# Backward loads on another queue, a gradient product with exchanged operands, a residual on GpSimd, and a tail in two steps

## The chip, the core and the metric

The kernel runs on one core of a Trainium2 chip. A core has five engines with instruction queues of their own, each worked off strictly in order: PE (TensorE, matrix products; its weight loads are shown apart as PEld), DVE (VectorE), ACT (ScalarE), POOL (GpSimd) and SP (SyncE, which computes nothing and issues DMAs). SP, ACT and POOL can issue DMAs; the transfers then run on the core's 16 DMA engines. An instruction that waits for a semaphore holds up everything behind it on its own engine. The metric is the device time of one launch in microseconds (us); lower is better. The profile is of one execution of the same program, with every instruction, semaphore and DMA packet.

## The reference

One block of a transformer, forward and backward, in bfloat16, with S = 2048 rows, width D = 448, 16 heads of 28, and F = 1792:

```
xn  = layernorm(x)
y   = x + MHA(xn; wqkv, wo) + SwiGLU(xn; w_gate, w_up, w_down)
out = y and, for a given grad_out, the gradients of
      x, wqkv, wo, w_gate, w_up, w_down
```

MHA is softmax attention over all rows with scale 28^-0.5; SwiGLU is (silu(xn w_gate) * (xn w_up)) w_down. The seven outputs are y, dx, d(wqkv), d(wo), d(w_gate), d(w_up), d(w_down), in that order.

## The kernel before

The program has three phases, one behind the other on every engine.

**Forward phase** (up to 655 us). For each of 4 groups of 4 heads, scores are made in transposed form by PE, exponentiated by ACT (L605) and multiplied with v. The whole feed-forward part, its gradients and the gradients of its weights are spread between these steps by a small work queue. What the backward phase needs goes to DRAM scratch: qT_d, kT_d, vT_d, dOT_d (per group, transposed), spq_d, spk_d, spo_d (per group, rows on partitions), hd_d (the three hidden tensors h, dgate, dup per row tile), wT_d and wqT_d (transposed weights). POOL issues nearly all of these stores.

**Backward phase** (655 to 1472 us). It runs over 512 units: 8 pairs of heads, 4 key blocks of 512, 16 query tiles of 128. One unit k is: scores on PE (L852), E = exp on ACT (L870), dP on PE for the unit before (L863), ds = dP * E on DVE (L881), and, three units later, the products that accumulate dk and dv on PE (acc_mm, L749). Eight units form a window W (so 64 windows); `pos` is a unit's place in its window. dq needs ds transposed: for 6 of a window's 8 units SP issues a transposing DMA dsT<-ds (L883), for the other two PE transposes (L776) and ACT or DVE copies out (L783). Two windows later dq_mm (L796) multiplies and DVE adds up (L808 to L814). ds lies in 8 rotating buffers (pool dsw), so a ds can be written only when the transposing DMA and the products of the unit eight before it are done.

Finished dk/dv blocks (dkv_o, L755) and dq blocks (dq_o, L814) are transposed back by a DMA from SP into dkv_sp and dq_sp (L762, L818) and stored to dqkv_d by POOL (L764, L821). These issues stand in a list `sp_later` and are emitted after the dsT of the next unit.

**Jobs.** Each window also carries at most one job of PE work from the list `jobs` (L650), in four portions at pos 1 to 4 between the unit's own products ("fillers"): 16 jobs "y" (a row tile of y: 4 + 14 products and one with the identity that adds x, L713 and L715), 32 jobs "dx" (a row tile of dgate or dup times the transposed weight, 14 products, L719) and 12 jobs "dwq" (4 chunks of 128 rows of d(wqkv), for each of the first three groups; 64 small products each, L677 and L682, with xn as the stationary operand and dkv_sp or dq_sp as the moving one). A job's result is copied out of PSUM by ACT (L728, L692) and stored by POOL (L730, L732); for a dwq job POOL first sorts the columns with 6 copies (L699). The fourth group's dwq products run at the end of the phase, in `last_dwq`.

**Loads of the phase**, all issued by SP, in the same queue as the transposing DMAs: the chunk ck of hd_d (and x_c) for the job two windows ahead, at pos 0 (L661, L663, L667; 3 buffers); at pos 4 parts of the next pair's qT and kT (8 parts of 128 KB over four windows, L553), of the next group's v_sp, vT, O_sp (6 parts of 256 KB over six windows, L564), and of the next weight W (parts of 224 KB, two a window, L540, one buffer).

**Tail** (1472 to 1548 us). Three `load_c` on SP bring the first pieces of pA_d, pB_d and dqkv_d (L937, L940), the rest is issued by ACT. After the last dwq products, 16 row tiles t of dx follow: 14 products on PE (L957, L959), a copy with a row sum on ACT (L963), the layer norm's gradient on DVE (L966 junk with a row sum, L970 bb, L972 cc), t1 on ACT (L975), t2 on DVE (L977), the addition of dy on POOL (L980) and the store by SP (L981).

Of the kernel before, what the change touches and what calls it, by code (L numbers as in the profile page):

```python
# [18 lines left out]
D = 448  # L19
# [18 lines left out]
def kernel(  # L38
# [493 lines left out]
    def load_w(nm, parts):  # L532
# [6 lines left out]
        q = pool if nm == "wd" else sp  # L539
        out = [lambda i=i: q.dma_start(out=t[:, i:i + step, :], in_=src[:, i:i + step, :])  # L540
# [5 lines left out]
    def load_pair(pr, parts):  # L546
# [6 lines left out]
        return [lambda i=i, dst=dst, r0=r0, src=src: sp.dma_start(  # L553
# [4 lines left out]
    def load_group(g, parts, kpool):  # L558
# [5 lines left out]
        return [lambda i=i, t=t, src=src: sp.dma_start(  # L564
# [65 lines left out]
    outp = cst.enter_context(tc.tile_pool(name="outp", bufs=2))  # L630
    ps_sd = cst.enter_context(tc.tile_pool(name="ps_sd", bufs=3, space=PSUM))
# [15 lines left out]
    chunk, dsp, dqacc = {}, {}, {}  # L647


    jobs = [None] + [("y", t) for t in range(NT)] + [None] + [("dwq", 0, c) for c in range(4)]  # L650
    jobs += [("dx", 0, t) for t in range(NT)] + [("dwq", 1, c) for c in range(4)]
    jobs += [("dx", 1, t) for t in range(8)] + [None] + [("dwq", 2, c) for c in range(4)]
    jobs += [("dx", 1, t) for t in range(8, NT)]

    def job_load(i):
# [3 lines left out]
        if j[0] == "y":  # L659
            t = ckp.tile([P, NFC + G, P], BF16, name="ck")  # L660
            sp.dma_start(out=t[:], in_=hd_d[j[1], :, :G + NFC, :])  # L661
            x = ckp.tile([P, D], BF16, name="x_c")
            sp.dma_start(out=x[:], in_=x_d[:, j[1], :])  # L663
            chunk[i] = (t, x)
        elif j[0] == "dx":
            t = ckp.tile([P, NFC + G, P], BF16, name="ck")
            sp.dma_start(out=t[:, :NFC], in_=hd_d[j[2], :, G + NFC * (1 + j[1]):G + NFC * (2 + j[1]), :])  # L667
            chunk[i] = t

    def dwq_mms(g, c, ps):  # L670

        out = []
        lhs = lambda t: xn_sp[:, t, c * P:(c + 1) * P]

        def kvm(t):
            for hp in range(2):
                pe.matmul(ps[:, hp * P:(hp + 1) * P], lhsT=lhs(t), rhs=dsp[2 * g + hp][0][:, t, :],  # L677
                          start=(t == 0 and hp == 0), stop=(t == NT - 1), skip_group_check=True)

        def qm(t):  # L680
            for hp in range(2):
                pe.matmul(ps[:, 256 + hp * 64:256 + hp * 64 + 64], lhsT=lhs(t),  # L682
                          rhs=dsp[2 * g + hp][1][:, t // 8, t % 4, t % 8 // 4, :],
                          start=False, stop=(t == NT - 1), skip_group_check=True)
        for f in (kvm, qm):
            out.append([lambda t=t, f=f: f(t) for t in range(NT)])
        return out

    def dwq_out(g, c, ps):
        d0, dn = DCH[c]  # L690
        o = outp.tile([P, 384], BF16, name="dwq_raw")
        act.copy(out=o[:], in_=ps[:, :384])  # L692
        z = outp.tile([P, 3, 4, DH], BF16, name="dwq_z")
        kv = o[:, :256].rearrange("p (h v j r) -> p h v j r", h=2, v=2, r=HP)
        for tq in range(3):
            for hp in range(2):
                src = (o[:, 256 + 64 * hp:320 + 64 * hp].rearrange("p (j r) -> p j r", r=HP) if tq == 0
                       else kv[:, hp, 2 - tq])
                pool.tensor_copy(out=z[:, tq, 2 * hp:2 * hp + 2, :], in_=src[:, :, :DH])  # L699
        pool.dma_start(  # L700
            out=out_2[d0:d0 + dn, :].rearrange("p (t c) -> p t c", t=3)[:, :, g * 4 * DH:(g + 1) * 4 * DH],
            in_=z[:dn].rearrange("p t h d -> p t (h d)"))

    def job_mms(i, ps):
        j = jobs[i]
        if j[0] == "dwq":
            return sum(dwq_mms(j[1], j[2], ps), [])
        if j[0] == "y":
            t, x = chunk[i]
# [303 lines left out]
```

## Time and profile before

| what | time |
|---|---|
| median of 3 runs (lowest, highest) | 1548.89 us (1547.53, 1555.15) |
| the profiled execution, and its span | 1549.43 us, 1547.7 us |
| granted PE clock, mean of the span | 0.978 |

Stages of the backward phase and the tail, from the busy time of each stretch. A window begins with the first E (L870) of its eight units; the period of a window is the distance to the next such start, read from the timeline of ACT.

| stage | windows | from, to (us) | length | PE busy | DVE busy | DMA, GB/s | shortest to longest window |
|---|---|---|---|---|---|---|---|
| y | 1 to 16 | 667.3, 883.8 | 216.5 | 193.5 | 169.1 | 205 | 12.23 to 16.67 |
| no job | 17 | 883.8, 894.6 | 10.8 | 9.3 | 10.4 | 187 | 10.8 |
| dwq, group 0 | 18 to 21 | 894.6, 952.4 | 57.8 | 48.9 | 42.6 | 203 | 11.85 to 17.18 |
| dx, gate | 22 to 37 | 952.4, 1156.0 | 203.6 | 189.1 | 169.8 | 202 | 11.76 to 16.01 |
| dwq, group 1 | 38 to 41 | 1156.0, 1204.0 | 48.0 | 46.1 | 42.4 | 193 | 11.88 to 12.15 |
| dx, up, first 8 | 42 to 49 | 1204.0, 1305.3 | 101.3 | 91.1 | 84.4 | 196 | 11.78 to 14.31 |
| no job | 50 | 1305.3, 1316.2 | 10.9 | 9.1 | 10.4 | 211 | 10.9 |
| dwq, group 2 | 51 to 54 | 1316.2, 1364.3 | 48.1 | 46.1 | 42.5 | 178 | 11.88 to 12.15 |
| dx, up, last 8 | 55 to 62 | 1364.3, 1459.6 | 95.3 | 92.0 | 85.0 | 195 | 11.78 to 12.15 |
| last window, start of the tail | 63 | 1459.6, 1494.5 | 34.9 | 28.1 | 14.1 | 248 | |
| rows of dx | | 1494.5, 1547.7 | 53.2 | 42.8 | 30.5 | 184 | |

"Busy" of PE is the time in which at least one product is under way. A window's period against the shortest ones of the same kind of job tells how much it lost; the DMA rate tells how much was moved in it. POOL is busy for 22.6 us of the 216.5 us of stage y and sits idle for the rest.

### The profile page before, as it was taken

What the parts mean: (1) busy time and instruction counts of PE and PEld (TensorE: products, weight loads), DVE (VectorE), ACT (ScalarE), POOL (GpSimd) and SP (SyncE); (2) the same over time, 40 slices, a digit from 0 to 9 for tenths busy, and PEclk for the clock granted to TensorE, in tenths of its full rate; (3) what the DMA queues carried; (4) which work ended last, traced back from release to release, by engine and by line L of the source; (5) the groups of instructions that cost most, each with busy time, mean ns of one, the idle gap of its engine ahead of it and who ended that gap; (6) DMA issues with size and microseconds to landing.
All of it is one profiled execution on the core that took longest, in us unless ns stands there. A gap on an engine that the chain in (4) does not pass through costs nothing.

```text
span 1547.7 us, 32024 instructions
## 1 busy us (share of the span) xinstructions
PE 1412.8 (91%) x12176; PEld 597.7 (39%) x12176; DVE 1099.4 (71%) x1421; ACT 1187.9 (77%) x1333; POOL 396.1 (26%) x664
## 2 busy tenths in 40 slices
PE   6899999999999989988988988989999889999987
PEld 3333333333333333433433444433335333543353
DVE  7654555656666657476877877878878789888935
ACT  6898988888788878676767867878778778888724
POOL 4341433343435355310110111111102101111033
PEclk9999999999999999999999999999999999999999
DMA  9985758767978689799999999999999999999994
GB/s 225 189 174 113 157 101 173 161 142 141 179 154 164 148 173 215 159 205 200 214 204 206 196 199 205 198 200 198 207 197 197 200 192 197 174 192 215 188 274 142
DMA packets 682106, 285.12 MB, mean 184 GB/s; under 512 B 637136, under 2 KB 650464, under 8 KB 681952
## 3 DMA queue, kind: packets, MB, share of 16 engines
q1 hardware_dynamic: 652016, 210.03, 74.6%
q0 software_dynamic: 25968, 64.53, 16.8%
q10 hardware_dynamic: 3968, 8.52, 1.6%
q8 instruction: 95, 1.56, 0.4%
q14 instruction: 59, 0.48, 0.1%
HBM read 67.34 MB, written 63.44 MB: 85 GB/s over the span
## 4 chain that ended last, share of the span: by engine, by line
PE 56%; DMA 13%; ACT 13%; DVE 8%; issue 6%; SPq 1%; POOL 1%; ACTq 0%; DVEq 0%; POOLq 0%
DMA dsT<-ds 9%; PE f_ps L357 7%; PE sd L852 6%; PE s_ps L600 6%; PE f_ps L383 6%; ACT E L870 5%; PE aux L719 4%; PE acc L749 4%; PE aux L796 4%; PE aux L776 4%; PE o_ps L582 4%; ACT eT L605 4%; DVE ds L881 3%; ACT dsT L783 3%; PE aux L713 3%
## 5 line engine op out<-in xcount | busy, mean ns | idle before, releaser
L881 DVE TENSOR_TENSOR ds<-sd,E 128x1024 bf16<-128x1024 f32 x512 | 611.4, 1220 | 137.5 <-DMA dsT<-ds 52.6
L870 ACT ACTIVATE E<-sd 128x1024 bf16<-128x1024 f32 x512 | 516.9, 1024 | 178.4 <-PE sd L863 140.2
L605 ACT ACTIVATE eT<-s_ps 128x1024 bf16<-128x1024 f32 x512 | 495.8, 1026 | 93.1 <-PE s_ps L600 89.6
L852 PE MATMUL sd<-kT,qT 32*128 32x512 bf16 x1024 | 201.8, 390 | 24.7 <-DVE ds L881 22.3
L863 PE MATMUL sd<-kT,qT 32*128 32x512 bf16 x1024 | 202.6, 389 | 23.6 <-ACT E L870 22.7
L749 PE MATMUL acc<-ds,v_sp 128*32 128x512 bf16 x1024 | 204.6, 395 | 0.7 <-DVE ds L881 0.7
L749 PE MATMUL acc<-E,O_sp 128*32 128x512 bf16 x1024 | 204.3, 395 | 0.2 <-ACT dkv_o L755 0.2
L600 PE MATMUL s_ps<-qT,kT 32*128 32x512 bf16 x1024 | 148.0, 386 | 7.8 <-ACT eT L605 5.6
L422 POOL DMA_DIRECT2D hd_d<-fT x168 | 126.9, 769 | 15.5 <-DVE fT L407 6.8
L383 PE MATMUL f_ps<-xnT,wgu 128*128 128x512 bf16 x448 | 118.8, 383 | 4.9 <-DVE w_sb L409 4.7
L764 POOL DMA_DIRECT2D dqkv_d<-dkv_o x64 | 39.3, 619 | 289.1 <-ACT dkv_o L755 287.3
L719 PE MATMUL aux<-W,ck 128*128 128x448 bf16 x448 | 108.4, 359 | 3.4
L852 PEld LDWEIGHTS <-qT 32*128 32x128 bf16 x1024 | 51.3, 91 | 154.1 <-issue 145.5
L582 PE MATMUL o_ps<-eT,v_sp 128*32 128x512 bf16 x1024 | 103.4, 394 | 0.6
L357 PE MATMUL f_ps<-xn_sp,f_sp 128*128 128x448 bf16 x448 | 99.1, 354 | 0.0
L749 PEld LDWEIGHTS <-O_sp 128*32 128x32 bf16 x1024 | 50.4, 94 | 113.4 <-issue 103.4
L600 PEld LDWEIGHTS <-kT 32*128 32x128 bf16 x1024 | 40.7, 91 | 137.7 <-issue 132.7
L776 PE MATMUL aux<-ident_bf,ds 128*128 128x128 bf16 x1024 | 79.4, 221 | 11.2 <-DVE dq_acc L808 5.8
L863 PEld LDWEIGHTS <-qT 32*128 32x128 bf16 x1024 | 65.4, 91 | 62.1 <-issue 58.2
L357 PEld LDWEIGHTS <-f_sp 128*128 128x128 bf16 x672 | 58.2, 98 | 77.4 <-issue 23.4
L776 PEld LDWEIGHTS <-ds 128*128 128x128 bf16 x1024 | 61.8, 98 | 39.8 <-issue 39.4
L395 DVE SCALAR_TENSOR_TENSOR g<-t_sb,f_ps 128x512 f32<-128x512 f32 x56 | 38.4, 686 | 53.3 <-ACT t_sb L393 53.2
(133 smaller groups left out, 1766.5 us busy)
## 6 DMA issues: line engine op xcount, KB each, us to landing
hd_d<-fT POOLq DMA_DIRECT2D x168, 128.0 KB, 4.4
ck<-hd_d SPq DMA_DIRECT2D x32, 448.0 KB, 4.4
ck<-hd_d SPq DMA_DIRECT2D x16, 576.0 KB, 5.1
dsT<-ds SPq DMA_TRANSPOSE x384, 4.2
dqkv_d<-dkv_o POOLq DMA_DIRECT2D x64, 64.0 KB, 3.8
dq_c<-dqkv_d ACTq DMA_DIRECT2D x5, 768.0 KB, 6.5
W<-wT_d SPq DMA_DIRECT2D x14, 224.0 KB, 3.6
out_dram<-dw_o POOLq DMA_DIRECT2D x28, 96.0 KB, 4.0
```

Source lines behind the costliest of these rows:

```text
L357: pe.matmul(acc[:, :D], lhsT=src[:, 12 * (t // 4) + 4 * wi + t % 4, :], rhs=rhs[:, t, :D], start=(t == 0), stop=(t == NT - 1))
L383: pe.matmul(st[name][:], lhsT=w(c), rhs=src[:, tsl, c, :], start=(c == 0), stop=(c == 3))
L582: pe.matmul(o_ps[HP * hh:HP * (hh + 1), :], lhsT=v[:, kt, HP * hh:HP * (hh + 1)], rhs=e[hh // 2][:, hh % 2, :], start=(kt == 0), stop=(kt ...
L600: pe.matmul(s_ps[:, j, :], lhsT=kT[r:r + HP, kt * P:(kt + 1) * P], rhs=qT[r:r + HP, qc * 512:(qc + 1) * 512], start=True, stop=True, tile_ ...
L605: act.activation(out=e[:], in_=s_ps[:], func=ACT.Exp, scale=SCALE)
L719: return [lambda n=n: pe.matmul(ps[:, :D], lhsT=t[:, n, :], rhs=w[:, n, :], start=(n == 0), stop=(n == NFC - 1)) for n in range(NFC)]
L749: pe.matmul(acc[r:r + HP, :], lhsT=src[:, qt, 64 * hp + HP * j:64 * hp + HP * j + HP], rhs=m[:, j, :], start=(qt == 0), stop=(qt == NT - 1 ...
L776: pe.transpose(ps[:, i, :], ds[:, i // 4, (i % 4) * P:(i % 4 + 1) * P], ident_bf[:])
L852: pe.matmul(s_ps[:, j, :], lhsT=q[HP * j:HP * j + HP, qt * P:(qt + 1) * P], rhs=kv[HP * j:HP * j + HP, kc * 512:(kc + 1) * 512], start=Tru ...
L863: pe.matmul(d_ps[:, j, :], lhsT=q[r:r + HP, qt * P:(qt + 1) * P], rhs=kv[r:r + HP, kc * 512:(kc + 1) * 512], start=True, stop=True, tile_p ...
L870: act.activation(out=E[k][:], in_=s_ps[:], func=ACT.Exp, scale=SCALE)
L881: dve.tensor_tensor(out=DS[k - 1][:], in0=d_ps[:], in1=E[k - 1][:], op=ALU.mult)
```

## The change

Five edits, made together.

1. Every load of the backward phase is issued by POOL and no longer by SP: ck and x_c, the pairs, the groups, and all weights. That includes the first pair and the first group, which are loaded near the end of the forward phase (L611).
2. dwq: for the first three groups, 3 jobs of 16 or 64 products each take the place of 4 jobs of 64. dkv_sp of one pair (c = 0, 1) or dq_sp of both pairs (c = 2) is the stationary operand, 448 columns of xn the moving one, so the result is the gradient transposed, 128 x 448. For c = 2 the operand is used in four pieces of 32 columns, each in its own column strip of PE. ACT copies the result to a bf16 tile with 64 zero columns, SP transposes it back by DMA, POOL sorts the columns (5 copies a group in all) and, with the third job, issues the four stores.
3. The list of jobs is 3 shorter; the windows without a job are now 0, 17, 40 and 60 to 63. The dwq jobs of group 2 now stand in windows 50 to 52, with 9 of the second "dx" jobs before them.
4. y: the product with the identity is left out. ACT copies PSUM to an fp32 tile, POOL adds x and writes the bf16 row that it then stores.
5. Tail: the last group's dwq is three results, each copied and transposed in turn after its products. In the loop over t, t2, the addition and the store (`finish`) of tile t - 1 follow t1 of tile t; the additions of the last three tiles are made by DVE.

```diff
@@ load_w, load_pair, load_group, job_load
-        q = pool if nm == "wd" else sp
-        out = [lambda i=i: q.dma_start(out=t[:, i:i + step, :], in_=src[:, i:i + step, :])
+        out = [lambda i=i: pool.dma_start(out=t[:, i:i + step, :], in_=src[:, i:i + step, :])
...
-        return [lambda i=i, dst=dst, r0=r0, src=src: sp.dma_start(
+        return [lambda i=i, dst=dst, r0=r0, src=src: pool.dma_start(
...
-            sp.dma_start(out=t[:], in_=hd_d[j[1], :, :G + NFC, :])
+            pool.dma_start(out=t[:], in_=hd_d[j[1], :, :G + NFC, :])
...
@@ jobs
-    jobs = [None] + [("y", t) for t in range(NT)] + [None] + [("dwq", 0, c) for c in range(4)]
-    jobs += [("dx", 0, t) for t in range(NT)] + [("dwq", 1, c) for c in range(4)]
-    jobs += [("dx", 1, t) for t in range(8)] + [None] + [("dwq", 2, c) for c in range(4)]
-    jobs += [("dx", 1, t) for t in range(8, NT)]
+    jobs = [None] + [("y", t) for t in range(NT)] + [None] + [("dwq", 0, c) for c in range(3)]
+    jobs += [("dx", 0, t) for t in range(NT)] + [("dwq", 1, c) for c in range(3)] + [None]
+    jobs += [("dx", 1, t) for t in range(9)] + [("dwq", 2, c) for c in range(3)]
+    jobs += [("dx", 1, t) for t in range(9, NT)]
@@ dwq_mms, dwq_out
         def kvm(t):
-            for hp in range(2):
-                pe.matmul(ps[:, hp * P:(hp + 1) * P], lhsT=lhs(t), rhs=dsp[2 * g + hp][0][:, t, :],
-                          start=(t == 0 and hp == 0), stop=(t == NT - 1), skip_group_check=True)
+            pe.matmul(ps[:, :D], lhsT=dsp[2 * g + c][0][:, t, :], rhs=xn_sp[:, t, :D],
+                      start=(t == 0), stop=(t == NT - 1))
         def qm(t):
-            for hp in range(2):
-                pe.matmul(ps[:, 256 + hp * 64:256 + hp * 64 + 64], lhsT=lhs(t),
-                          rhs=dsp[2 * g + hp][1][:, t // 8, t % 4, t % 8 // 4, :],
-                          start=False, stop=(t == NT - 1), skip_group_check=True)
+            for h in range(4):
+                pe.matmul(ps[HP * h:HP * (h + 1), :D],
+                          lhsT=dsp[2 * g + h // 2][1][:, t // 8, t % 4, t % 8 // 4, HP * (h % 2):HP * (h % 2 + 1)],
+                          rhs=xn_sp[:, t, :D], start=(t == 0), stop=(t == NT - 1),
+                          tile_position=(0, HP * h), skip_group_check=True)
+        return [lambda t=t: (kvm if c < 2 else qm)(t) for t in range(NT)]
...
+        w = dwq_w[c % 2]
+        act.copy(out=w[:, :D], in_=ps[:, :D])
...
+        def later():
+            sp.dma_start_transpose(out=o[:], in_=w[:])
+            parts = [(0, 0, 4, 0)] if c == 2 else [(2, 2 * c, 2, 0), (1, 2 * c, 2, 64)]
+            for tq, h0, n, c0 in parts:
+                pool.tensor_copy(out=z[:, :, tq, h0:h0 + n, :],
+                                 in_=o[:, :, c0:c0 + HP * n].rearrange("p c (h r) -> p c h r", r=HP)[:, :, :, :DH])
+            if c < 2:
+                return
+            for i, (d0, dn) in enumerate(DCH):
+                pool.dma_start(
...
+        sp_later.append(later)
@@ y
-            out.append(lambda: pe.matmul(ps[:, :D], lhsT=ident_bf[:], rhs=x[:], start=False, stop=True))
...
+        if j[0] == "y":
+            y = outp.tile([P, D], FP32, name="y_sb")
+            act.copy(out=y[:], in_=ps[:, :D])
+            pool.tensor_tensor(out=o[:], in0=y[:], in1=chunk[i][1][:], op=ALU.add)
+        else:
+            act.copy(out=o[:], in_=ps[:, :D])
@@ tail
+        for c, (ps, m) in enumerate(last_dwq):
+            for f in m[12 if c < 2 else 0:]:
+                f()
+            dwq_out(3, c, ps)
+            while sp_later:
+                sp_later.pop(0)()
...
+        def finish(t, t1, cc):
+            t2 = wk.tile([P, D], FP32, name="t2")
+            dve.scalar_tensor_tensor(out=t2[:], in0=xn_sp[:, t, :D], scalar=cc[:, 0:1], in1=t1[:],
+                                     op0=ALU.mult, op1=ALU.add)
+            dx = wk.tile([P, D], BF16, name="dx")
+            add = pool if t < NT - 3 else dve
+            add.tensor_tensor(out=dx[:], in0=t2[:], in1=dy_t[:, t, :], op=ALU.add)
+            sp.dma_start(out=out1_d[:, t, :], in_=dx[:])
...
+            if t > 0:
+                finish(t - 1, *held)
+            held = (t1, cc)
+        finish(NT - 1, *held)
```

## The prediction

> **What bounds the kernel now.** I read the page first (busy shares, chain, groups, DMA issues), then the start of every eighth L870 for the window periods, then the waits of the slow windows, then SP's queue as a timeline.
>
> ```profile
> DMA dsT<-ds 9%; PE f_ps L357 7%; PE sd L852 6%; PE s_ps L600 6%; PE f_ps L383 6%; ACT E L870 5%; PE aux L719 4%; PE acc L749 4%; PE aux L796 4%; PE aux L776 4%; PE o_ps L582 4%; ACT eT L605 4%; DVE ds L881 3%; ACT dsT L783 3%; PE aux L713 3%
> L881 DVE TENSOR_TENSOR ds<-sd,E 128x1024 bf16<-128x1024 f32 x512 | 611.4, 1220 | 137.5 <-DMA dsT<-ds 52.6
> dsT<-ds SPq DMA_TRANSPOSE x384, 4.2
> ```
>
> PE leads with 91% busy, yet the largest single item of the chain is a transfer, the transposing DMA dsT. DVE's ds waits 52.6 us for it: the buffer that ds wants has not been read yet. The chain in order of time places those pieces in windows that the table above shows as long. An undisturbed window takes 12.5 us with a y job, 11.9 with dx (11.78 and 12.05 in turn), 12.0 with dwq, 10.85 with none. Against that, stage y loses 216.5 - 16 x 12.5 = 16.5 us, the dwq of group 0 57.8 - 48.0 = 9.8, the first dx stage 203.6 - 16 x 11.92 = 12.9, the first half of the second 101.3 - 8 x 11.92 = 5.9, the rest nothing. Sum: 45 us of stalls. SP's queue in one slow window:
>
> ```profile
> 799.86 0.79 SPq L661 DMA_DIRECT2D ck<-hd_d  x1
> 800.75 0.38 SPq L663 DMA_DIRECT2D x_c<-in_A_x_dram  x1
> 801.22 6.54 SPq L883 DMA_TRANSPOSE dsT<-ds  x3
> 807.86 1.24 SPq L762 DMA_TRANSPOSE dkv_sp<-dkv_o  x1
> 809.14 1.22 SPq L553 DMA_DIRECT2D qT<-dOT_d  x2
> 810.46 3.98 SPq L883 DMA_TRANSPOSE dsT<-ds  x3
> 814.54 0.53 SPq L661 DMA_DIRECT2D ck<-hd_d  x1
> ```
>
> There is no gap: SP issues without a pause and is late. From one ck to the next it needs 14.7 us where PE needs 12.5. Three dsT take 3.98 us (1.3 each) away from ck, 6.54 behind it: an issue behind a 576 KB load is stretched by 2.6 us. An undisturbed window, late in the phase, where nothing but ck is loaded:
>
> ```profile
> 1379.82 0.53 SPq L667 DMA_DIRECT2D ck<-hd_d  x1
> 1380.44 4.98 SPq L883 DMA_TRANSPOSE dsT<-ds  x3
> 1385.83 1.60 SPq L762 DMA_TRANSPOSE dkv_sp<-dkv_o  x1
> 1387.53 2.77 SPq L883 DMA_TRANSPOSE dsT<-ds  x2
> 1390.36 1.30 SPq L818 DMA_TRANSPOSE dq_sp<-dq_o  x1
> 1391.75 1.52 SPq L883 DMA_TRANSPOSE dsT<-ds  x1
> ```
>
> Even here SP is taken for nearly the whole window. So SP's queue is the second bound, just below PE, and each load on it tips a window over.
>
> **Edit 1, loads to POOL.** It moves 48 ck, 16 x_c, 16 W, 56 pair and 18 group parts, 154 issues, and 7 of the first pair and group. What stays on SP per window: 6 dsT x 1.35 us (1.29 the median, plus the gap) + 0.75 dkv/dq x 1.3 = 9.1 us, for windows of 11.9 to 12.4. That is 2.8 us of slack where the slow windows lacked 1 to 4, and the backlog that starts each slow stretch doesn't form. Rest on POOL: one issue there takes 0.57 (112 KB) to 1.10 us (the one large load that POOL issues already), so the fullest y window costs 1.0 + 0.6 + 2 x 0.6 + 0.6 = 3.4 us on top of about 1.4 now: no bound. On POOL's queue the loads pass behind stores that wait for ACT (L730, L764) and in front of others; ck is due two windows later, row_o and dkv_o are rewritten two jobs later, so some 12 us of lateness are covered. The 7 early loads join POOL's stores of the forward phase, whose late landing held L407 for 10.4 us in all: I take 0, bounds -1 to +2.
>
> The transfers themselves remain, and this is the uncertain part. How a POOL load and SP's transposes share the DMA engines is visible only once, at the end of the forward phase, where 1568 KB are loaded by POOL:
>
> ```profile
> 640.00:648.00 8.00, 8.00 (x56) 3.10 (x53) 1.25 (x2) 6.33 (x7) 1.89 (x3) 1.00 1.01 269
> ```
>
> The DMA engines carry 269 GB/s there (last column), against about 200 in every stage of the backward phase, slow or not. A transpose issued in the load's last 2 us landed after 2.9 us, as against 2.5 undisturbed. So the engines have some room, and the rate of about 200 looks like that of one queue worked off in order. I let four fifths of the 45 us go: **-36** (bounds 0 and -45).
>
> The Trainium skill, "DMA: Bandwidth & Descriptors", section "Issuing engines are not separate DMA queues", speaks against this: transfers interleave on the same engines whoever issues them, and spreading the issues saves only the sequencer's time. The same page, "Queues, rings and completion order", has each DMA engine take turns between queues packet by packet, which would let a transpose past a load. By the first alone the stretched issues would stay and the time would be that of the first rival below; by the second, the forecast. The row at 640 us leans to the second without settling it.
>
> **Edit 2 and 3, dwq.** Twelve windows of 12.02 (144.2 us) become six with 16 products of 448 columns, three with 64 column-strip products and three more empty ones. A y window is 0.59 us longer than a dx window for 5 more products, so one more filler costs 0.12 us: 16 against 14 makes 12.16. The strips are nearest to L796:
>
> ```profile
> L715 PE MATMUL aux<-x_c,ident_bf 128*128 128x448 bf16 x16 | 5.6, 352 | 0.0
> L796 PE MATMUL aux<-dsT,vT 128*32 128x512 bf16 x1024 | 75.4, 395 | 0.6
> L699 POOL COPY dwq_z<-dwq_raw 128x56 bf16<-128x56 bf16 x96 | 17.8, 250 | 82.5 <-ACT dwq_raw L692 78.6 <-DMA out_dram<-dwq_z 3.9
> ```
>
> 75.4 / 1024 = 74 ns each, so 64 take 4.7 us of PE against 2.6 for 14 full products (0.187 each, from 5 in 0.93): as much as 11 more fillers, 13.2 us at most; if the strips overlap four deep, 12.2. I take 12.5. 6 x 12.16 + 3 x 12.5 + 3 x 10.85 = 143.0: **-1.2** (bounds -2.1 and +0.9). SP gets 9 more transposes of about 1.25 us, one in nine windows that load no ck: inside the slack. POOL waits in its queue for each of them, 4 to 8 us, with the next ck and the last W part behind it; these have 8 us and more. If that cover fails see the second rival.
>
> **Edit 4, y.** 18 fillers for 19 in 16 windows: 16 x 0.12 = **-1.9** (bounds: +1.1 if ACT's fp32 copy costs 0.07 more, as L470's 0.60 against L728's 0.53, and sits on the path; -5.6 with L715's whole duration). The addition on POOL is like L980, 1.03 us, off the path. In the tail L980 delays DVE in one place only:
>
> ```profile
> 1522.15 1.03 POOL L980 TENSOR_TENSOR dx<-t,dy_t 128x448 bf16<-128x448 f32 x1 [1.70 <-DVE t L977]
> 1522.52 0.09 DVE L966 DVE_READ_ACCUMULATOR junk<-sd,xn_sp 128x1 f32 x1
> 1522.52 0.67 DVE L970 SCALAR_TENSOR_TENSOR bb<-s,rstd 128x1 f32<-128x1 f32 x1
> ```
>
> bb, with both operands in SBUF, ends when the addition ends (0.67 against 0.16 alone); junk (L966), with one operand in PSUM, keeps its 0.62 beside it. ds also reads PSUM, so I charge it nothing.
>
> **Edit 5, tail.** Start: the last dq_sp lands at 1487.3 and 6.8 us of small products and PSUM copies follow before L957 at 1494.1. Now only 32 strips follow (2.4 us, to 1489.7); then the first dq_c, landed at 1491.8, is next, so L959 starts at 1491.8 instead of 1494.5: -2.7 (0 to -4.4). Middle: a tile takes 2.73 us, and its parts are DVE's junk, bb until POOL ends, cc, 0.85 waiting for t1, t2; PE alone needs 2.65 (1497.13 to 1499.78). With t2 one tile later the wait goes: 10 x 0.08 = -0.8. End: from the last product (1537.8) to POOL's last addition (1545.0) are 7.2 us; anew g_sb 0.74, junk 0.7, bb and cc 0.3, then on DVE t2 and addition of tile 14 beside t1 (1.35), t2 and addition of tile 15 (1.35), gaps 0.2: 4.6, so -2.6. Sum **-6.1** (bounds +2, if the transposes and POOL's sorting delay the first tiles, and -8).
>
> **Sum.** 36 + 1.2 + 1.9 + 6.1 = 45.2; span 1547.7 - 45.2 = 1502.5. The profiled execution lies 1.7 above its span, the median 0.5 below that execution: 1503.7, so **1504 us**. All good ends give 1547.7 - 45 - 2.1 - 5.6 - 8 - 1 = 1486, +1.2 = 1487.
>
> **Rivals.** (a) The DMA engines are the wall and the stalls stay: 1538.5 + 1.2 = 1540 us. For it: the DMA share is above 1 in every stage and the rate about 200 in slow and clean windows alike. Against: 269 above, 248 where the tail loads.
> (b) POOL's in-order queue makes loads late: ck or the last W part waits behind a dwq transpose or a row that ACT hasn't copied. Two weight changes at up to 8 us: 1520. Against: two windows of lead.
> (c) Slower. POOL's loads no longer stand in line, and take their time from the transposes just when these are due, in clean windows too. ds has 8 buffers, 8 x 1.49 = 11.9 us of cover; transposes land after 4.2 us now, 7.8 at most. From the point where issue and landing together pass about 10 us, each of the 48 windows with a ck loses that load's transfer, 4.1 - 2.5 = 1.6 us: +77, the old stalls being in it: 1504 + 77 = 1581. Against: the same bytes, merely in another order.
> (d) The clean windows had hidden waits as well and get shorter: 20 us more, 1484.
>
> **Chances.** Forecast 62% (1488 to 1526), (a) 15%, (b) 10%, (c) 9%, (d) 4%. The range 1487 to 1541 leaves out (c), (d) and the upper part of (a). Half a per cent, about what a measurement of this kernel can tell, is 7.7 us: faster than 1541.1 are the forecast, (b), (d) and half of (a), 0.83; within it the other half, 0.07; slower (c) and some more, 0.10.
>
> **What would show it.** Right: no window of the phase over 13 us, ds waiting for dsT under 10 us in all, gaps in SP's queue, y windows near 12.4, the empty windows at 10.85, L959 starting within 2 us of the first dq_c's landing, the last addition 5 us behind the last product. Wrong: dsT landing later than 4.2 us in the median with DVE still waiting for it (a, c); PE waiting for ck or W (b); strip windows over 13.

## The result, and the profile after

| | before | after |
|---|---|---|
| median (lowest, highest) | 1548.21 us (1545.40, 1555.15) | 1615.22 us (1598.10, 1643.27) |
| span of the profiled execution | 1547.7 us | 1596.3 us |
| granted PE clock, mean | 0.978 | 0.959 |
| ds waiting for dsT, sum (times, longest) | 52.6 us (38, 3.5) | 110.1 us (48, 8.8) |
| dsT from issue to landing, median, latest | 4.2, 7.8 us | 4.5, 15.8 us |

The change makes the kernel slower: time after by time before is 1.039, with a 95% interval of 1.030 to 1.048. The forecast was 1504 us. The longest run after was executed in a slower state of the chip (granted clock 0.938), which the medians hold and the ratios leave out, here and in e1 below. The profiled execution (1598.1 us) is the shortest run after, so the 48.6 us between the spans account for most of the 67 us between the medians and not for all.

First the same lines of the page as in the prediction: the chain, the group of ds, the transfers, and (new) the two queues with packets, MB and their share of 16 engines' span. Of the DMA issues the columns are KB each and median us to landing.

```profile
q1 hardware_dynamic: 639200, 166.37, 63.7%
q0 software_dynamic: 37664, 109.76, 29.2%
...
DMA dsT<-ds 14%; PE f_ps L357 7%; PE sd L864 6%; PE f_ps L383 5%; PE s_ps L599 5%; PE aux L727 5%; ACT E L882 4%; PE acc L761 4%; ACT eT L604 4%; PE aux L808 4%; PE o_ps L581 3%; PE aux L788 3%; DVE ds L893 3%; ACT dsT L795 2%; PE sd L875 2%
...
L893 DVE TENSOR_TENSOR ds<-sd,E 128x1024 bf16<-128x1024 f32 x512 | 610.6, 1219 | 184.5 <-DMA dsT<-ds 110.1
...
ck<-hd_d POOLq DMA_DIRECT2D x32, 448.0 KB, 5.9
...
dsT<-ds SPq DMA_TRANSPOSE x384, 4.5
```

The same transfer leads the chain, with 14% instead of 9, and ds (now L893) waits twice as long for it. The median landing hardly moved (4.2 to 4.5); the late ones did. ck now needs 5.9 us where SP's needed 4.4.

Taking the excess of each window over the undisturbed one of its kind (y 12.51 before and 12.42 after, dx 11.92, dwq 12.05, none 10.85), the 48.6 us come apart: stalls from 44.4 to 98.1 (+53.7), shorter undisturbed windows -5.0 (y -1.4, three windows without a job -3.6), tail -2.1, start of the phase +2.2.

One of the worst windows as a timeline (start, length, engine, line, count; in brackets the idle time before and what ended it):

```profile
929.43 1.21 SPq L700 DMA_TRANSPOSE dwq_o<-dwq_w  x1
930.73 18.21 SPq L895 DMA_TRANSPOSE dsT<-ds  x6
949.05 1.23 SPq L700 DMA_TRANSPOSE dwq_o<-dwq_w  x1
...
932.00 0.69 POOL L703 COPY dwq_z<-dwq_o 128x224 bf16<-128x224 bf16 x2 [12.20 <-DMA dwq_o<-dwq_w]
932.63 0.54 POOL L671 DMA_DIRECT2D ck<-hd_d  x1
933.16 1.06 POOL L552 DMA_DIRECT2D kT<-vT_d  x2
934.20 0.58 POOL L563 DMA_DIRECT2D vT<-spk_d  x1
934.77 1.08 POOL L539 DMA_DIRECT2D W<-wT_d  x2
...
947.94 2.36 DVE L893 TENSOR_TENSOR ds<-sd,E 128x1024 bf16<-128x1024 f32 x2 [8.46 <-DMA dsT<-ds]
...
949.22 0.61 PE L864 MATMUL sd<-kT,qT 32*128 32x512 bf16 x2 [8.20 <-DVE ds L893]
```

POOL waited 12.2 us for a transposed dwq, then issued six loads in 3.2 us, 1.4 MB. SP's queue holds nothing but transposes now, and yet six of them take 18.2 us (3.98 for three before). The dsT issued at 933.47 landed at 947.8, with the last of the loads; ds and PE stood for 8 us.

Busy time by stretch of the same kernel: PE, PEld, DVE, ACT, POOL, then granted PE clock, DMA share, GB/s.

```profile
930.00:938.00 8.00, 6.47 (x71) 2.46 (x68) 6.55 (x7) 5.48 (x7) 3.84 (x8) 1.00 1.02 192
938.00:947.00 9.00, 2.45 (x38) 1.27 (x37) 1.22 (x1) 2.59 (x3) 0.00 (x0) 0.78 1.13 123
947.00:960.00 13.00, 10.59 (x124) 4.19 (x123) 10.05 (x10) 7.35 (x9) 3.53 (x7) 0.76 1.01 205
1281.50:1305.30 23.80, 22.85 (x224) 9.70 (x220) 21.21 (x21) 19.51 (x22) 3.45 (x6) 1.00 1.04 193
```

The DMA share is the time of all packets by that of 16 engines; it is above 1 where packets overlap. In the stall the DMA engines were busier (1.13) and moved less: 123 GB/s, where the undisturbed stretch of the last line moves 193. The prediction read 269 GB/s beside one POOL load at 640 us; with loads and transposes side by side the rate goes the other way. The row at 640 us couldn't show that, for nearly all that moved there was POOL's own. The queues of that stretch in the kernel before (q0 is POOL's, q1 the one with the transposes; packets, MB, share):

```profile
q0 software_dynamic: 571, 1.97, 87.2%
q1 hardware_dynamic: 728, 0.18, 13.8%
```

In the tail the additions on POOL no longer delay bb (0.15 us), a tile takes 2.65 us and the last addition ends 4.1 us behind the last product (7.2 before). But the rows of dx came to a stop near their start:

```profile
1535.76 0.42 SPq L949 DMA_DIRECT2D pab<-pA_d  x1
1536.30 0.36 SPq L949 DMA_DIRECT2D pab<-pB_d  x1
1537.70 0.32 SPq L952 DMA_DIRECT2D dq_c<-dqkv_d  x1
1538.67 12.96 SPq L700 DMA_TRANSPOSE dwq_o<-dwq_w  x3
...
1549.78 0.53 ACT L693 CAST dwq_w<-sd 128x448 bf16<-128x448 f32 x1 [15.32 <-DMA dwq_o<-dwq_w]
```

The three new transposes stand on SP behind the tail's first loads; ACT's third copy into dwq_w (two buffers) waited 15.3 us for the first of them, and g_sb of the first row behind it.

### The profile page after: what moved, and what is told of

Same layout as the page of the kernel before. It is cut to its first block, busy times and chain, and to the rows that moved or that the text cites. A ratio compares the mean times of both kernels' runs of the same rounds, so it can differ in the third digit from the quotient of the medians.

```text
span 1596.3 us, 30644 instructions
## 1 busy us (share of the span) xinstructions
PE 1420.5 (89%) x11520; PEld 567.3 (36%) x11520; DVE 1096.2 (69%) x1424; ACT 1188.6 (74%) x1329; POOL 486.6 (30%) x764
## 4 chain that ended last, share of the span: by engine, by line
PE 55%; DMA 20%; ACT 12%; DVE 7%; issue 5%; SPq 0%; POOL 0%; DVEq 0%; ACTq 0%; POOLq 0%
DMA dsT<-ds 14%; PE f_ps L357 7%; PE sd L864 6%; PE f_ps L383 5%; PE s_ps L599 5%; PE aux L727 5%; ACT E L882 4%; PE acc L761 4%; ACT eT L604 4%; PE aux L808 4%; PE o_ps L581 3%; PE aux L788 3%; DVE ds L893 3%; ACT dsT L795 2%; PE sd L875 2%
## 5 line engine op out<-in xcount | busy, mean ns | idle before, releaser
L893 DVE TENSOR_TENSOR ds<-sd,E 128x1024 bf16<-128x1024 f32 x512 | 610.6, 1219 | 184.5 <-DMA dsT<-ds 110.1
L864 PE MATMUL sd<-kT,qT 32*128 32x512 bf16 x1024 | 206.5, 399 | 69.5 <-DVE ds L893 66.8
L875 PE MATMUL sd<-kT,qT 32*128 32x512 bf16 x1024 | 207.4, 398 | 23.4 <-ACT E L882 22.7
L761 PE MATMUL acc<-ds,v_sp 128*32 128x512 bf16 x1024 | 208.8, 403 | 0.7 <-DVE ds L893 0.7
L761 PE MATMUL acc<-E,O_sp 128*32 128x512 bf16 x1024 | 208.5, 403 | 0.4 <-ACT dkv_o L767 0.4
L422 POOL DMA_DIRECT2D hd_d<-fT x168 | 126.9, 771 | 16.8 <-DVE fT L407 4.9
L727 PE MATMUL aux<-W,ck 128*128 128x448 bf16 x448 | 111.6, 367 | 5.6 <-DMA W<-wT_d 2.0
L808 PE MATMUL aux<-dsT,vT 128*32 128x512 bf16 x1024 | 77.8, 411 | 0.7
L788 PEld LDWEIGHTS <-ds 128*128 128x128 bf16 x1024 | 63.3, 100 | 37.9 <-issue 37.4
```

The lines of the kernel that those rows point to most:

```text
L727: return [lambda n=n: pe.matmul(ps[:, :D], lhsT=t[:, n, :], rhs=w[:, n, :], start=(n == 0), stop=(n == NFC - 1)) for n in range(NFC)]
L761: pe.matmul(acc[r:r + HP, :], lhsT=src[:, qt, 64 * hp + HP * j:64 * hp + HP * j + HP], rhs=m[:, j, :], start=(qt == 0), stop=(qt == NT - 1 ...
L788: pe.transpose(ps[:, i, :], ds[:, i // 4, (i % 4) * P:(i % 4 + 1) * P], ident_bf[:])
L864: pe.matmul(s_ps[:, j, :], lhsT=q[HP * j:HP * j + HP, qt * P:(qt + 1) * P], rhs=kv[HP * j:HP * j + HP, kc * 512:(kc + 1) * 512], start=Tru ...
L875: pe.matmul(d_ps[:, j, :], lhsT=q[r:r + HP, qt * P:(qt + 1) * P], rhs=kv[r:r + HP, kc * 512:(kc + 1) * 512], start=True, stop=True, tile_p ...
L893: dve.tensor_tensor(out=DS[k - 1][:], in0=d_ps[:], in1=E[k - 1][:], op=ALU.mult)
```

## The experiments

Ratios are to the kernel before, run beside each on the same chip, with 95% intervals. "Stalls" is the sum of the windows' excess as above, from the profiled execution, like the two columns behind it; that of e1 was 21 us longer than its median, so no sum is given for it. e6 and e14 leave out most of ck's transfer and serve as measurements only.

| run | median, us | ratio | stalls, us | ds for dsT, us | latest dsT, us |
|---|---|---|---|---|---|
| e1 edit 1 alone | 1618.25 | 1.042 (1.037 to 1.046) | | 131.6 | 21.3 |
| e2 all but edit 1 | 1562.98 | 1.006 (1.002 to 1.011) | 63.1 | 89.3 | 8.8 |
| e3 after, loads paced | 1576.85 | 1.016 (1.011 to 1.021) | 74.0 | 77.8 | 16.5 |
| e4 ck and x_c on POOL | 1590.51 | 1.026 (1.022 to 1.030) | 83.2 | 88.0 | 13.1 |
| e5 ck and x_c on ACT | 1579.60 | 1.019 (1.014 to 1.023) | 59.1 | 14.2 | 10.7 |
| e9 e4, paced | 1564.38 | 1.011 (1.007 to 1.014) | 56.1 | 47.2 | 11.5 |
| e15 e9, ck in parts | 1551.57 | 1.001 (0.999 to 1.003) | 31.4 | 31.6 | 8.4 |
| e6 small ck on SP | 1524.39 | 0.984 (0.980 to 0.988) | 15.9 | 18.1 | 8.0 |
| e14 small ck on POOL | 1519.61 | 0.981 (0.979 to 0.983) | 11.1 | 13.9 | 7.6 |
| e7 dwq alone | 1566.19 | 1.010 (1.007 to 1.014) | 61.4 | 88.8 | 9.1 |
| e8 y and two-step tail | 1542.14 | 0.996 (0.993 to 0.998) | 40.6 | 52.1 | 8.4 |
| e10 after, 10 ds | 1628.01 | 1.049 (1.043 to 1.054) | 125.1 | 106.5 | 19.0 |
| e11 e8, 12 ds | 1548.53 | 1.000 (0.998 to 1.002) | 39.0 | 16.8 | 7.8 |
| e12 e2, 10 ds, 3 dwq_w | 1561.89 | 1.007 (1.004 to 1.010) | 56.5 | 37.4 | 8.2 |
| e13 e8, loads spread | 1543.79 | 0.996 (0.995 to 0.998) | 44.0 | 67.9 | 8.1 |
| e16 e8, third ds by PE | 1532.09 | 0.989 (0.986 to 0.991) | 26.7 | 0 | 7.0 |
| e17 e16, copy by DVE | 1528.62 | 0.987 (0.984 to 0.989) | 27.8 | 2.8 | 6.8 |
| e18 e17 in 12 windows | 1529.09 | 0.987 (0.984 to 0.989) | 22.1 | 20.0 | 7.5 |

### Which edit: e1, e2

e1 is the kernel before with the loads moved; e2 the kernel after with them moved back:

```diff
-            sp.dma_start(out=t[:], in_=hd_d[j[1], :, :G + NFC, :])
+            pool.dma_start(out=t[:], in_=hd_d[j[1], :, :G + NFC, :])
...
```

> The kernel before with edit 1 alone: every load of the backward phase on POOL, nothing else changed. Theory B (bursts): POOL, which nothing paces, issues the loads of one or two windows within a few us, and a transposing DMA issued meanwhile lands only with the last of them. Then this alone is slower than before: 1580 to 1610 us, with landings of dsT of 12 us and more in stages y and dx too. Theory W: the bursts come only from POOL's new waits for the dwq transposes, which are not in this kernel: 1505 to 1545 us. Theory S (sharing): any load on POOL's queue takes the transposes' time, however it is spread: 1590 to 1620 us, with nearly every window with a ck longer than 13 us.

> The changed kernel with its loads back on SP, the other four edits kept. B, S and W alike say that the loss is in edit 1 or in what edit 1 meets, so this is not slower than before: the PE work saved (about 3 us) and the tail (2 us in the changed kernel) remain, the old stalls of about 44 us come back: 1540 to 1550 us. If it is over 1560, one of the other edits costs time by itself and the blame on the loads is wrong.

Edit 1 alone costs all that the change costs; theory W, which needs POOL's waits for a dwq transpose, falls, since e1 has none. The other four edits together are no gain either (1.006), which is taken up below.

### How POOL's loads do it: e3, e4, e5, e9, e15

e3 keeps after's loads on POOL and holds each behind a tiny POOL copy of a ds two units old, one load in a unit. e4 moves ck and x_c alone.

```diff
+    def pace(k):
+        if k >= 2:
+            pool.tensor_copy(out=pace_t[:], in_=DS[k - 2][:, 0, 0:1])
...
-                for lst, n in ((pload, 2), (gload, 1), (wload, 2)):
-                    for f in lst[:n]:
-                        f()
-                    del lst[:n]
+            for lst, at in ((pload, (3, 5)), (gload, (4,)), (wload, (2, 6))):
+                if lst and pos in at:
+                    pace(k)
+                    lst.pop(0)()
```

> The changed kernel, loads on POOL, but each of them held back by a small POOL copy that reads the ds of two units before, and spread over the window: ck at pos 0, W at pos 2 and 6, pair parts at pos 3 and 5, the group part at pos 4. B: no burst in stages y and dx, their stalls (75 us in the changed kernel) fall below 20; some 15 us stay around the dwq windows where POOL waits for transposes: 1510 to 1545 us. S: no change, 1590 to 1620 us. W: little change in stage y, most stalls stay around the dwq jobs: 1580 to 1610 us.

> The kernel before with ck and x_c alone on POOL; pairs, groups and weights stay on SP. B: POOL has one load of 448 to 688 KB a window and can't run ahead by more than one more, so few bursts; SP is relieved of 0.6 to 1.1 us of issues and of the 2.6 us by which a ck stretches the next issues: 1505 to 1540 us. S: every window with a ck loses about 1.5 us: 1580 us or more.

Theories B (bursts) and S (sharing) are both half right. Pacing brings the loss from 3.9% to 1.6%, so the bursts of several loads matter; but one ck in a window, with every other load on SP, still costs 2.6%. In e4's timeline:

```profile
1186.50 9.76 SPq L883 DMA_TRANSPOSE dsT<-ds  x6
...
1197.47 19.40 SPq L883 DMA_TRANSPOSE dsT<-ds  x6
...
1198.02 0.68 POOL L667 DMA_DIRECT2D ck<-hd_d  x1
```

A single ck of 448 KB, issued by POOL 0.55 us behind a transpose, doubles the time that SP needs for the next six. It landed after 12.0 us itself. In the packet records of that stretch eight packets of 7168 B, from 1205.05 on, are under way for 3364 to 3374 ns each, while most others of the same load take 272 to 333; all eight end within 0.02 us, at 1208.42. Hardly anything else moves meanwhile (columns as above, the last is GB/s):

```profile
1205.30:1208.40 3.10, 2.40 (x44) 1.34 (x41) 0.00 (x0) 2.66 (x4) 1.47 (x4) 1.00 0.46 37
```

Of the transposes 63 packets in a us begin here (194 of 256 B), where an undisturbed stretch of the kernel before (1281.5 to 1305.3) has 583. The transposes issued at 1197.47 and 1199.17 landed at 1210.0 and 1212.3. What held the packets is not shown: the records don't name the engine that a packet ran on.

Is it POOL's queue, or any second queue, or the instant? e5 has ACT issue ck and x_c; e9 is e4 with ck held at pos 0 of its window by `pace`; e15 is e9 with ck in four parts of 128 to 160 KB, one in a unit:

```diff
+            for lo in range(0, G + NFC, 5):
+                hi = min(lo + 5, G + NFC)
+                cload.append(lambda t=t, lo=lo, hi=hi: pool.dma_start(out=t[:, lo:hi], in_=hd_d[j[1], :, lo:hi, :]))
...
+            if cload and pos in (0, 2, 4, 5, 6):
+                pace(k)
+                cload.pop(0)()
```

> The kernel before with ck and x_c issued by ACT, one load a window on a queue that is neither SP's nor POOL's. Theory S (two queues that run side by side get out of step, whoever issues): as with ck alone on POOL, dsT's latest landing over 12 us, 1575 to 1600 us. Rival P (it is POOL's software queue with its 4096 B packets that disturbs the transposes): dsT's latest landing below 9 us, and 1535 to 1560; ACT gives 64 issues of some 0.5 us, about one half of a us a window, which it can hide because it isn't the bound.

> The kernel before with ck and x_c on POOL, as in the run with ck alone, but each held at the start of its window by a small POOL copy of a ds made two units earlier, so that it starts when ACT's ck started in the run with ck on ACT. Theory Q (POOL's own queue disturbs the transposes, whenever it starts): 1575 to 1595 us, dsT's latest landing over 12 us. Rival I (the instant decides: POOL starts a ck right behind a stored row, in the middle of the transposes): 1545 to 1560, latest landing below 11, as with ACT.

> The kernel before with ck and x_c on POOL, paced by ds as in the run with ck paced, but each ck in four parts of 128 KB or so, one in a unit, instead of one of 448 or 576 KB. If a large load on POOL's queue holds the transposes because its 16 engines get out of step over several us, small parts let them pass: dsT's latest landing under 9 us, 1545 to 1557 us. If any load beside the transposes costs by its bytes, as the paced one: 1558 to 1570; if by its number of packets and starts, over 1570.

e5's time hit theory S's range for another reason: ds waits only 14 us for dsT. Its undisturbed dx windows are 12.79 and 12.52 us instead of 12.05 and 11.78, 0.74 longer: ACT, which was thought to have room for the issues, has none. That is 32 x 0.74 = 24 of its 59 us of "stalls", for the 32 windows that load a ck for dx; why an issue of 0.33 us costs 0.74 is open. e9 lies between its two ranges: the instant is worth 26 us (e4 to e9), and 16 us stay. e15 takes these away too:

```profile
ck<-hd_d POOLq DMA_DIRECT2D x96, 128.0 KB, 4.0
ck<-hd_d POOLq DMA_DIRECT2D x48, 160.0 KB, 4.3
...
dsT<-ds SPq DMA_TRANSPOSE x384, 4.7
```

The same bytes on the same queue beside the same transposes, and the time is that of before, with the latest dsT at 8.4 us. Packets of the large loads' sizes (4608 and 7168 B on POOL's queue, 3584 and 4608 on SP's and ACT's, 4096 and 5120 in parts) that took over 2 us, between 660 and 1450 us: 1 before, 68 in e4, 27 in e9, 14 in e5, 0 in e15. So POOL's queue by itself is not at fault: a large piece that starts beside the transposes is, or so many bytes at once; e15 makes the pieces smaller and spreads them over the window, and no run parts the two. The transposes' own packets (256 B) are not free of it either: 34 took over 2 us before, 37 in e4, 3 in e9 and 48 in e15. These counts don't follow the time; those of the large packets do from e4 to e9 to e15. That small pieces let the transposes pass agrees with what the Trainium skill says in "DMA: Bandwidth & Descriptors", section "Queues, rings and completion order": each engine takes turns between queues, a packet at a time. A packet took up to 3.4 us here (e4), so the rule need not help a transpose beside large packets.

Yet e15 is no faster than before, though SP has 64 issues fewer to make. Its profiled execution, 4.8 us below its median, does have fewer stalls (31.4 us against 44.4); its first window starts 5.6 us later, though, and its tail is 4.2 us longer. So in the windows up to 13 us may be the issues or ck's place in SP's queue. Where, then, is the rest of the bound?

### The transfers, not the issues: e6, e14, e13

e6 loads one block of each ck from SP, e14 from POOL:

```diff
-            sp.dma_start(out=t[:], in_=hd_d[j[1], :, :G + NFC, :])
+            sp.dma_start(out=t[:, :1], in_=hd_d[j[1], :, :1, :])
...
-                out.append(lambda n=n, rhs=rhs: pe.matmul(ps[:, :D], lhsT=t[:, n, :], rhs=rhs,
+                out.append(lambda n=n, rhs=rhs: pe.matmul(ps[:, :D], lhsT=t[:, 0, :], rhs=rhs,
```

> The kernel before with one block of 32 KB loaded of each ck instead of 14 or 18; all products of a job use that block. It leaves out most of ck's transfer and keeps every issue and every product. If the 44 us of stalls before come from ck's transfers (an issue behind a 448 or 576 KB load is stretched, and lands late), the long windows go: 1503 to 1520 us. If they come from the time that SP's issues take by themselves, little changes: 1535 to 1550.

> The kernel before with one block of 32 KB loaded of each ck, as in the run with the small ck on SP (the rest of the transfer left out), and with ck and x_c issued by POOL. Together with that run it parts the time of SP's issues from that of the transfers. If freeing SP of 64 issues is worth what the prediction took, most of the 16 us of stalls that are left there go: 1508 to 1516 us. If SP's issues are only long because the engines behind them are full, or POOL's x_c of 112 KB disturbs too, no gain or a loss: 1522 to 1540.

Without ck's bytes, but with all of SP's issues, 24 us go (1.6%, 1.2 to 2.1) and with them most of the stalls; the time is 4 us above the range given. Taking the issues off SP as well (e14) brings 5 us more (0.3%; the intervals just overlap). In the lists of waits of e6 and of e14 (sum, times, longest):

```profile
DVE ds L881 <- DMA dsT<-ds: 18.1, 18, 1.9
```

```profile
DVE ds L881 <- DMA dsT<-ds: 13.9, 12, 2.9
```

Most of the stalls of the kernel before are thus ck's transfer, and SP's lack of gaps is largely its shadow: an issue is long because of what is under way behind it. e6 alone doesn't tell whether ck fills the engines or stands in front of the transposes in SP's queue; that e15, with the same bytes off that queue, keeps 31.4 us and e14, without them, 11.1 speaks for the first. That the issues themselves bring little is what the Trainium skill's page "DMA: Bandwidth & Descriptors", section "Issuing engines are not separate DMA queues", has: spreading the issues saves only the issuer's time. Here that time was worth some 5 us of 1549 (e6 to e14), not clear of the noise.

e13 leaves the bytes and spreads the pairs over 7 windows instead of 4, the groups over 12 instead of 6 (on top of e8):

```diff
-                for lst, n in ((pload, 2), (gload, 1), (wload, 2)):
+                for lst, n in ((pload, 1 + (W % 8 == 0)), (gload, W % 2), (wload, 2)):
```

> The kernel with y's residual by POOL and the tail in two steps, and on SP one part of a pair in a window instead of two (two in the first), one part of a group in two windows instead of one in each. The same bytes, spread over 7 and 12 windows instead of 4 and 6. If the stalls come from windows in which ck, pair and group stand together, they fall from 41 to 10 to 25 us: 1515 to 1530 us. If every window with a ck is full already, so that spreading only moves the backlog, 1538 to 1550.

Nothing is gained: the stalls are 44.0 against 40.6 of e8. So spreading only moves the backlog; that a window with a ck has no room to work it off is the reading, not shown by itself.

### A version that is faster: e16, e17, e18

If the engines are full in the windows that load the next pair, a transpose taken out of these is worth more than a load moved. e16 is e8 with a third ds transposed by PE in 24 windows; e17 has DVE copy it out; e18 does it in 12 windows:

```diff
+    third = lambda W: W % 8 < 4 and W < 48
...
-            if qi not in TQ:
+            if qi not in TQ and not (qi == 2 and third((k - 1) // UW)):
...
+        if pos == 7 and W < NW and third(W):
+            pe_transpose(W, 2)
+            tr_out(act)
```

> The kernel with y's residual by POOL and the tail in two steps, and in the first four windows of each of six pairs (24 windows, those in which the next pair is loaded) a third ds transposed by PE instead of by DMA: 0.55 us of PE and 1.0 us of ACT more in each, one transposing DMA of about 1.3 us fewer on SP and on the engines. If the transfers of these windows are the wall that makes the 41 us of stalls, the stalls fall by 4 x 1.3 us a stretch, some 25 us, for 24 x 0.6 = 14 us of longer windows: 1527 to 1537 us. If the stalls have another cause, only the cost stays: 1553 to 1560.

> The run with a third ds transposed by PE in 24 windows, with the copy out of PSUM made by DVE (0.68 us) instead of ACT (1.02). There no ds waited for a transposing DMA any more, and each of the 24 windows was 1.2 us longer, about what ACT's copy takes. If ACT's copy is that price, the windows are 0.5 to 0.8 longer instead: 1515 to 1525 us. If PE's eight transposes and their place set it, no change: 1528 to 1536.

> The same in 12 windows (the first and third of each pair) instead of 24. If one transposing DMA less in every other loaded window is enough for SP's queue to catch up, half the price and no stalls: 1510 to 1520 us. If the wall comes back, half of the 41 us of stalls return: 1528 to 1545.

e16 is 1.1% faster than before, and the chain of its page no longer has dsT among its 15 largest pieces:

```profile
PE f_ps L357 7%; PE sd L857 7%; PE s_ps L600 6%; PE f_ps L383 6%; ACT E L875 6%; PE aux L718 6%; PE acc L753 5%; ACT eT L605 5%; PE aux L801 5%; PE aux L781 5%; ACT dsT L788 4%; PE aux L713 4%; PE o_ps L582 4%; PE sd L868 3%; PE f_ps L180 2%
...
dsT<-ds SPq DMA_TRANSPOSE x360, 4.1
```

No ds waits for dsT at all. 24 transposes fewer of 384 remove all of e8's 41 us; what is left (26.7) is the price, 24 windows that are 1.2 to 1.4 us longer (13.44, 12.96, 13.23, 12.96 where 12.05 and 11.78 are undisturbed). In e17 they are 1.0 longer, and the window behind each four 0.3 longer where e16's was 0.2 shorter: over five windows the price falls only from 4.7 to 4.3 us, so ACT's copy was a small part of it, and the time is in the range that was given for no change. In e18 the price halves and 20 us of waits come back, so the time is e17's, 9 us above the range without stalls: one transpose less in every other loaded window is not enough. e17 and e18 are the fastest here that do the whole work, 1.3% below before.

### The other edits: e7, e8, e10, e11, e12

e7 is before with edits 2 and 3 and the dwq part of the tail, e8 before with the y edit and `finish`.

> The kernel before with the exchanged operands of dwq alone (loads on SP, tail with its transposes). By the floors of the windows -1 to -4 us; if its nine more transposes a phase on SP's queue make the windows after them long, as the run with the loads back on SP suggests, +5 to +20: 1553 to 1568. Without that 1540 to 1552.

> The kernel before with y's residual by POOL and the tail in two steps. By the prediction's terms -1.9 for y and -3.4 for the middle and end of the tail, so 1542 to 1546 us. If POOL's addition delays ds, or the y stage's long windows move, within 3 us of before.

e8 gains 0.4% (0.2 to 0.7), as its terms said. e7 costs 1.0%: its undisturbed windows are no longer than forecast, but the stalls grow by 17 us. SP's queue behind the dwq windows of group 2, where the kernel before lost nothing:

```profile
1332.52 1.21 SPq L700 DMA_TRANSPOSE dwq_o<-dwq_w  x1
1333.82 2.64 SPq L891 DMA_TRANSPOSE dsT<-ds  x2
1336.51 0.62 SPq L671 DMA_DIRECT2D ck<-hd_d  x1
1337.23 5.02 SPq L891 DMA_TRANSPOSE dsT<-ds  x3
1342.31 1.23 SPq L552 DMA_DIRECT2D kT<-vT_d  x2
1343.63 1.26 SPq L891 DMA_TRANSPOSE dsT<-ds  x1
1345.00 2.13 SPq L700 DMA_TRANSPOSE dwq_o<-dwq_w  x1
```

One more transpose, beside ck and a part of a pair, and the queue has no gap: windows 51 to 56 take 12.8, 13.8, 13.2, 13.8, 12.5 and 12.1 us. The dwq windows were taken to load no ck, but two of every three load one, for the job two windows on.

More ds buffers were to ride the late transposes out:

```diff
-    dsw = ast.enter_context(tc.tile_pool(name="dsw", bufs=8))
+    dsw = ast.enter_context(tc.tile_pool(name="dsw", bufs=12))
```

> The changed kernel with 10 buffers of ds instead of 8 and nothing else. If the late transposes cost time only through the ds that still waits to be read, each of the some 20 stretches loses up to 2 x 1.5 us less: 1565 to 1595 us. If something else stretches the windows (the clock, PE waiting for loads), no change: 1605 to 1625.

> The kernel before with y's residual by POOL, the tail in two steps and 12 buffers of ds instead of 8. If the stalls of the kernel before are bursts that a longer cover rides out, 4 x 1.5 = 6 us of each of some eight stretches go: 1505 to 1525 us. If SP's queue is too slow on average in these stretches and only the start is put off, 1530 to 1540.

> The changed kernel with its loads back on SP, 10 buffers of ds and three of dwq_w. With three dwq_w the copy of the last result no longer waits in the tail for the first transpose, so the tail from the start of the last window is some 4 us shorter than in the run with the loads on SP, 81 to 82 us; with two more ds the stalls of 63 us fall to 40 to 50: together 1538 to 1552 us. If the exchanged dwq keeps its cost in spite of the longer cover, over 1555.

None gains: e10 and e11 miss both of their ranges, and e12 is in the one for no gain (over 1555). In e11 ds waits 16.8 us for dsT instead of 52.1, and the sum of stalls is the same (39.0 for 40.6): fewer and longer; window 18 alone takes 23.7 us. There PE stands for another transfer of SP's queue:

```profile
909.57 0.96 PE L682 MATMUL aux<-dq_sp,xn_sp 128*128 128x64 bf16 x15 [9.72 <-DMA dq_sp<-dq_o]
```

A deeper buffer lets the backlog grow until the next user of the queue comes due, here a dwq job with its dq_sp. The first window is also 7.8 us longer than in e8: a ds waits 9.5 us there for the store of dwd_sb to end, whose buffer the larger pool lies on. e10 is not better than after, probably for the same reason: ds waits 106.5 us for dsT where it waited 110.1 after, and the stalls are 125.1 us. In e12 the third dwq_w does free ACT in the tail, and the wait moves one engine on:

```profile
1512.82 1.72 POOL L703 COPY dwq_z<-dwq_o 128x224 bf16<-128x224 bf16 x4 [17.79 <-DMA dwq_o<-dwq_w]
...
1520.19 1.46 POOL L708 DMA_DIRECT2D out_dram<-dwq_z  x2 [0.30 <-POOL dwq_z L703]
...
1524.46 3.17 POOL L969 TENSOR_TENSOR dx<-t,dy_t 128x448 bf16<-128x448 f32 x3
```

POOL waits 17.8 us for the same transposes, its additions of the first rows wait behind it, and DVE waits 8 us for those. The tail is 87.9 us, no shorter than before (88.0).

## Why the prediction was wrong

**The bound.** "SP issues without a pause and is late", so "SP's queue is the second bound": the reading of the rows was right, the cause was not. e6 leaves every issue and loses most of the stalls; e14 takes the issues away too and wins 5 us more. The transfers are most of the bound, which was rival (a), put at 15% (its price, 1540 us, had no loss either), and e4, e9 and e15, which all free SP of 64 issues, show no gain in time.

**Edit 1, -36: the step that failed.** Two things in it. "2.8 us of slack where the slow windows lacked 1 to 4" counted undisturbed issues of 1.35 us; beside POOL's loads an issue takes 3 us (18.2 for six). And from one row at 640 us, where a transpose issued in a load's last 2 us landed after 2.9 us, it was taken that POOL's loads let transposes past; that row held 1.97 MB of POOL's and 0.18 of the transposes' queue. In e1 the term is +65 (4.2%, 3.7 to 4.6), not -36. The mechanism is rival (c)'s: the loads "take their time from the transposes just when these are due". But (c) priced it as each load's own transfer, 1.6 us in each of 48 windows, clean ones too. Measured, most windows of dx with nothing but a ck stay at 12.05 and 11.78, and 24 windows lose 0.7 to 10 us each. The argument against (c), "the same bytes, merely in another order", was the error: the order is what costs. In SP's one queue a load and a transpose follow each other; from two queues they are under way together, and there packets of 7168 B took 3.4 us while the transposes stood nearly still (e4). How the one holds the other is open.

**Rival (b)** had POOL making loads late. In the window at 930 us POOL did stand 12.2 us behind a dwq transpose, but the loads behind it came as a burst that delayed transposes; e1 loses as much without that wait.

**dwq, -1.2.** By the undisturbed windows the term is -2.6: 6 x 12.13 for the kv jobs (12.24 and 12.02 in turn), 3 x 12.08 for the strips (12.5 was taken; they are below its lower bound of 12.2) and 3 x 10.85 without a job make 141.6 against 144.2. "One in nine windows that load no ck: inside the slack" is what failed: the slack did not exist, and the whole edit costs 16 us (e7, 10 to 22).

**y, -1.9,** measured -1.4 by the windows (12.42 on average against 12.51). ds beside POOL's addition is undisturbed, as assumed.

**Tail, -6.1,** mis-sized: after -2.1. Middle and end hold (e8's tail is 83.2 us against 88.0, -4.8 for -3.4), and the first product with dq_c (L981 of the kernel after) started 0.1 us after that had landed. The start failed: the transposes behind 4 MB of loads on SP (three dq_c and four parts of pab) hold ACT for 15.3 us. The bound "+2, if the transposes and POOL's sorting delay the first tiles" named it, with a size too small.

**What stays open:** what holds a large packet for over 3 us, which no record shows; whether the size of the pieces or their spread over the window made e15 faster than e9; and whether the rest between e9 and e5 is the queue's kind or the few us between the instants at which POOL and ACT issue. The loss of e1 and of the other four edits add up to more (4.8%) than that of the change (3.9%), within the interval.

## What to carry to other kernels

A queue that is issued without a gap can be the shadow of the transfers behind its issues: before moving issues to another engine, make the transfers small and keep the issues, and see which of the two the time follows. Loads that stood in line with latency-bound transfers on one queue were paced by it; on a queue of their own they need a pace and small pieces (128 KB here, not 448), and even then the bytes remain. Where the transfers are the bound, work taken off the engines (a transpose in 16 done by PE) was worth 0.9% on top of e8 (0.9868 / 0.9956); a deeper buffer or a wider spread only moved the wait to the next user of the same queue.

## What the hardware showed unexpectedly

- Loads and transposing DMAs in two queues moved 123 GB/s at a DMA share of 1.13; an undisturbed stretch of the same kernel moved 193 at 1.04.
- One packet of 7168 B can take 3.4 us instead of 0.28; eight at once did, all ending within 0.02 us (e4).
- After PE stood for 8.2 us (949.2 us in the kernel after), a pair of products took 0.61 us instead of 0.39 for the next 4.3 us, with the granted clock at 0.76 in the stretch from 947 to 960: by 4.3 x (1 - 0.39 / 0.61) this stall cost some 1.5 us more than itself.
- An issue of ck on ACT takes 0.33 us in the records but lengthens a window by 0.74.
